# Attention and MLP on one Trainium2 core: batch 0's order, w_in's first half in blocks, two loads moved

## The chip, the core and the metric

The kernel runs on one core of one Trainium2 chip. A core has five engines that each run their own list of instructions in order: TensorE (PE in the profile; its weight loads are listed as PEld), VectorE (DVE), ScalarE (ACT), GpSimd (POOL) and SyncE (SP). They meet only where one waits for another's semaphore. Loads and stores are DMAs, issued by POOL, SP or ACT and carried out by the core's 16 DMA engines. The metric is the device time of one execution in microseconds (us); lower is better.

## The reference

Eight batches of eight heads, 512 local and 32 global tokens, head size 64. A local query sees the local keys within 32 positions and all 32 global keys; a global query sees all keys. The result of each head goes through a gated two-layer MLP of width 512, 2048, 512.

```
s_g = scale * q_g @ [k_g, k_l].T          ; out_g = softmax(s_g) @ [v_g, v_l]
s_l = [scale * q_l @ k_g.T, where(|i-j| <= 32, scale * q_l @ k_l.T, -1e9)]
out_l = softmax(s_l) @ [v_g, v_l]
x = concat([out_g, out_l], axis=2) -> (8 * 544, 512)
h = x @ w_in ; out = (h * sigmoid(1.702 * h)) @ w_out
```

## The kernel before

The types are bf16 with sums in f32 banks. Attention works on a *quad*: four heads of one batch side by side, so a batch has two quads; `a` is the first and `c` the second. A quad's work is a list of steps, each a method:

- `Tk`, `Tq` (L302, L309): VectorE turns the k and q loads into the layout that TensorE needs; `ext` puts the global queries beside them. q and k are loaded by `load(b, us, names)` (L74), where `us` names the quads of batch b.
- `B(rnd)` (L328): matmuls that write the band's bias into the banks of the scores; `S(rnd)` (L338): the score matmuls on top, in two rounds; `X(rnd)` (L375): ScalarE's exponentials into `E[rnd]`; `gg`, `K`, `XK`, `eg`: the same for the global tokens.
- `ekU(unit)`, `U(unit)` (L418, L429): three units of matmuls of the exponentials with ones (unit 0, the row sums) and with the two halves of v; `R` (L460) turns the row sums into reciprocals on VectorE; `XL(h)` (L470) multiplies units 1 and 2 by them and writes `xL`, the MLP's input. `Gm` and `G` do it for the global queries.
- `h_mm(i, fc, hp, kcs)` (L584): the MLP's first layer, one of 16 column blocks `fc` of w_in, in four parts `kc` of the contraction; parts 0 and 1 need quad a's xL, parts 2 and 3 quad c's. `h_step` adds the gate on ScalarE and VectorE (`th`, then `gT`); `o_mm` is the second layer.
- `zero(n, ...)` (L644): matmuls of zeros that add nothing to a bank; fillers.

Batches 1 to 7 use `Wide`, a variant of the quad with masks in place of the bias matmuls (`M`).

The order of the program (L651 on) is written out by hand, and each engine runs its share in this order. Batch 0 has nothing to overlap with but its own two quads. From L727 on, the h matmuls of batch 0 run, and later batches put their attention between the o matmuls of the batch before.

The loads of the early part are issued by POOL: L143 to L146 and L225 to L226 first, then `load_rest` (L248), called at L663, in this order: v of batch 0, constants, w_in in four blocks, w_out's quarters 1 and 0, the masks (on POOL itself), batch 1's first quad, its global tokens, its second quad, its global v, w_out's quarters 2 and 3, batch 2's first quad, batch 1's v, more global tokens. A w_in block of the before is one half of the columns (1,024) of one half of the rows; the rows of h part 0 and 1 are the first, those of 2 and 3 the second. Batch 2's second quad, v and later batches are loaded from L777 on.

`step` (L150), `ident`, `band` and `bias` (L195 to L197) are constants that a POOL select and three VectorE instructions make; the first bias matmuls need them.

Of the kernel before, what the change touches and what calls it, by code (L numbers as in the profile page):

```python
# [12 lines left out]
F32 = mybir.dt.float32  # L13
# [7 lines left out]
def kernel(  # L21
# [12 lines left out]
    nc = tc.nc  # L34
# [10 lines left out]
    NQ = B * 2  # L45
# [11 lines left out]
    consts = ctx.enter_context(tc.tile_pool(name="consts", bufs=1))  # L57
# [16 lines left out]
    def load(b, us=(0, 1), names="qk"):  # L74
        if b not in loaded:
            loaded[b] = (ld.tile([128, 2, 16 * D], BF16, name="rk"),
                         ld.tile([128, 2, 16 * D], BF16, name="rq"))
        s = slice(us[0], us[-1] + 1)
        for name in names:
            dst, src = ((loaded[b][0], kf), (loaded[b][1], qf))[name == "q"]  # L80
            nc.gpsimd.dma_start(out=dst[:, s], in_=src[b][:, s])
# [8 lines left out]
    def load_v(b):  # L90
        if b == 2:
            nc.gpsimd.memset(v_view(b, 5)[:, :, :, :, D:], 1.0)
        vt = v_view(b, 5).rearrange("p u j c d -> p (u j) c d")
        vs, vg = (x[b].rearrange("h s d -> s h d") for x in (v_l, v_g))
        for c in range(5):
            n = 128 if c == 2 else 96
            nc.gpsimd.dma_start(out=vt[0:n, :, c, :D], in_=vs[FIRST[c] : FIRST[c] + n])  # L97
            if c != 2 and b > 1:
                nc.gpsimd.dma_start(out=vt[96:128, :, c, :D], in_=vg)  # L99

    def load_vg(b):
        nc.gpsimd.dma_start(out=v_view(b, 5).rearrange("p u j c d -> p (u j) c d")[96:128, :, 0, :D],
                            in_=v_g[b].rearrange("h s d -> s h d"))

    def spread_vg(b):
        vt = v_view(b, 5).rearrange("p u j c d -> p (u j) c d")
        nc.vector.tensor_copy(vt[96:128, :, 1, :D], vt[96:128, :, 0, :D])
        nc.vector.tensor_copy(vt[96:128, :, 3:5, :D],
                              vt[96:128, :, 0:1, :D].to_broadcast([32, 8, 2, D]))
# [6 lines left out]
    def load_turned(eng, out_, in_):  # L116
        eng.dma_start(out=out_[32:128], in_=in_[0:96])
        eng.dma_start(out=out_[0:32], in_=in_[96:128])

    def load_g(lo, hi, names="kq"):  # L120
        for name, dst, src in (("k", rkg, kgf), ("q", rqg, qgf)):
            if name in names:
                nc.gpsimd.dma_start(out=dst[:, lo:hi, :], in_=src[:, lo:hi, :])
# [10 lines left out]
    def cast_g32(name, t):  # L134
        nc.vector.tensor_copy(t[:, 0:2, :D], g32[name])
# [5 lines left out]
    halves = (slice(0, 8 * D), slice(8 * D, 16 * D))  # L141
    load_g32("q", qgf)
    for f, eng in zip(halves, (nc.scalar, nc.sync)):  # L143
# [5 lines left out]
    nc.vector.memset(warm, 0.0)  # L149
    step = consts.tile([128, 289], BF16)  # L150
    nc.vector.memset(step, 1.0)
    nc.gpsimd.affine_select(
        out=step, in_=step, pattern=[[1, 289]], compare_op=ALU.is_ge,
        fill=0.0, base=-97, channel_multiplier=-1,
# [6 lines left out]
    def set_consts():  # L161
        nc.gpsimd.memset(ones32, 1.0)
        nc.gpsimd.memset(bd, 0.0)
        for j in range(4):
            r = (j + 1) % 4
            nc.gpsimd.memset(bd[32 * r : 32 * r + 32, j, :], 1.0)
        nc.gpsimd.memset(rvg[:, :, D:], 1.0)
        for i in range(2):
            nc.gpsimd.memset(v_view(i, 4 + i)[:, :, :, :, D:], 1.0)

    w_in_sb = wts.tile([128, 2, NKC, d_ff // 2], BF16)
    w_out_sb = wts.tile([128, FC, d_model], BF16)
    w_in_r = moe_w_in.rearrange("(u p h) f -> u p h f", u=2, h=2)
# [7 lines left out]
    for i in range(4):  # L181
        qt = consts.tile([128, 24, 32], F32, name="q%d" % i)
        nc.vector.memset(qt[:, 0:4, :], 0.0)
        nc.vector.memset(qt[:, 20:24, :], 0.0)
        qtiles.append(qt)

    WIN = ((0, 10), (6, 12), (14, 12), (22, 10))
    mask = consts.tile([128, 2, MW], BF16)
# [26 lines left out]
    def make_mask(part):  # L215
        rnd, at, t0, t1, nr, base, rows = part
        src = band[:, base : base + 16 * nr].rearrange("p (r t) -> p t r", t=16)
        nc.gpsimd.tensor_copy(mask_at(rnd, at, t1 - t0, nr)[0:rows], src[0:rows, t0:t1])

    def mask_rest():  # L220
        nc.gpsimd.memset(mask, 1.0)
        nc.gpsimd.memset(mask_at(0, 248, 16, 12)[96:128, :, 0:4], 0.0)
        nc.gpsimd.memset(mask_at(1, 236, 16, 12)[96:128, :, 8:12], 0.0)

    load(0, (1,), "kq")  # L225
    load_turned(nc.gpsimd, rvg[:, 0:2, :D], vgf[:, 0:2])  # L226

    qgT = consts.tile([128, NQ, 40], F32)
    nc.vector.memset(qgT[:, :, 32:], 0.0)
    kgT = consts.tile([128, NQ, 32], F32)  # L230
    def transpose_g(lo, hi, names="qk"):
        for name, dst, s in (("q", qgT, rqg), ("k", kgT, rkg)):
            if name not in names:
                continue
            nc.vector.transpose(dst[:, lo:hi, :32], s[:, lo:hi].bitcast(F32))

    def load_v2(b):
        vp = v_l[b].rearrange("(u h) (c p) d -> u p h c d", u=2, p=128)
        for u in range(2):
            for p in (slice(0, 64), slice(64, 128)):  # L240
                nc.gpsimd.dma_start(out=v_view(b, 4)[p, u, :, :, :D], in_=vp[u, p])

    def load_w_out(g4):
        nc.gpsimd.dma_start(
            out=w_out_sb[:, 4 * g4 : 4 * g4 + 4, :].rearrange("p (g e) m -> p g (e m)", e=2),
            in_=w_out_r[:, 2 * g4 : 2 * g4 + 2, :])

    def load_rest():  # L248
        load_v2(0)
        set_consts()  # L250
        half = d_ff // 2
        for part in range(2):
            for u in range(2):
                nc.gpsimd.dma_start(out=w_in_sb[:, part, 2 * u : 2 * u + 2, :],
                                    in_=w_in_r[u][:, :, part * half : (part + 1) * half])
        load_w_out(1)
        load_w_out(0)
        mask_rest()
        for part in MASKS:
            make_mask(part)  # L260
        load(1, (0,))
        load_g(2, 4)
        load(1, (1,))
        load_vg(1)
        load_w_out(2)
        load_w_out(3)
        load(2, (0,))
        load_v(1)
        load_g(4, 8)

# [10 lines left out]
    def bank(pair, j):  # L281
        return pair[j // 2][:, j % 2, :]
# [296 lines left out]
    def width(i):  # L579
        return TB if i < B else B * Sg  # L580
# [3 lines left out]
    def h_mm(i, fc, hp, kcs):  # L584
        for kc in kcs:
            nc.tensor.matmul(hp[:, : width(i)], lhsT=w_in_c[:, fc // 8, kc, fc % 8 // 2, :, fc % 2],  # L586
                             rhs=(xL[i] if i < B else xG)[:, kc, :],
                             start=(kc == 0), stop=(kc == NKC - 1))
# [53 lines left out]
    a, c = Quad(0), Quad(1)  # L642

    def zero(n, ps, m=128, w=512):  # L644
        for _ in range(n):
            nc.tensor.matmul(ps[:m, :w], lhsT=warm[:, :m], rhs=warm[:, :w], start=False, stop=False, skip_group_check=True)

    def cast_k(f):
        nc.scalar.activation(rk[:, 0, f], k32[:, f], AF.Copy)

    cast_k(halves[0])  # L651
    cast_g32("q", rqg)
    transpose_g(0, 2, "q")
    a.ext((0, 1), True)
    cast_k(halves[1])
    a.Tk(0, 8)
    a.Tq(0, 8)
    a.Tk(8, 16)
# [4 lines left out]
    load_rest()  # L663
    a.B(0)
    a.B(1, split=True)
    zero(34, a.bk[1][3], 32, 32)
    a.S(0, added=True, part=0)
    a.S(0, added=True, part=1)
    a.X(0)
    a.S(1, split=True, added=True)  # L670
    zero(3, a.bk[1][3])
    a.X(1)
    c.Tk()
    c.ext()
# [5 lines left out]
    c.gg()  # L680
    c.X(0)
    a.eg()
    a.ekU(0)
    a.U(0)
    a.R()
    c.K()
    c.XK()
    a.ekU(1)
    a.U(1)
    a.XL(0)  # L690
    c.B(1, js=(0, 1))
    c.B(1, js=(2, 3))
    c.S(1, added=True)
    c.X(1)
    a.ekU(2)
    a.U(2)
    a.XL(1)
    a.Gm()
    gTs[0] = moe.tile([128, FC, TB], BF16, name="gT")
    pt = pts[0] = spair()  # L700
    c.ekU(0)
# [3 lines left out]
    c.U(1)  # L705
    c.ekU(2)
    c.U(2)
    c.eg()
    for fc in range(4):
        h_mm(0, fc, bank(pt, fc), (0, 1))  # L710
    c.XL(0)
    c.XL(1)
    for kc in (2, 3):
        for fc in range(4):
            h_mm(0, fc, bank(pt, fc), (kc,))
# [21 lines left out]
    nq = {b: (Wide(2 * b), Wide(2 * b + 1)) for b in (1, 2)}  # L737
    a, c = nq[1]
# [11 lines left out]
    a.S(1)  # L750
    a.X(1)
    spread_vg(1)
    nq[2][0].Tq()
    a.M(1)
    nq[2][0].Tk()
    osteps(0, (1, 2), (2, 2))
# [17 lines left out]
    a.G()  # L774
    transpose_g(4, 6)
    nq[2][0].ext(nc.gpsimd)
    load(2, (1,))  # L777
    load_v(2)
    load(3)
    osteps(0, (3, 2), (3, 3))  # L780
    a, c = nq[2]
# [4 lines left out]
    for fc in range(FC):  # L786
        if fc < 2:
            h_act(1, fc, hps[fc])
        else:
            h_step(1, fc)  # L790
        if fc == 1:
            nq[1][1].G()
        if fc == 10:
            a.S(0)
            a.X(0)
            a.M(0, nc.gpsimd)
            load_v(3)
            load(4)
            load_g(8, NQ)
# [101 lines left out]
```

## Time and profile before

| what | us |
|---|---|
| three runs, median (lowest to highest) | 299.2 (299.19 to 299.46) |
| the profiled execution, its own time | 299.52 |
| its span in the profile | 297.7 |
| TensorE busy | 291.9 |
| VectorE busy | 219.1 |
| ScalarE busy | 165.0 |
| GpSimd busy | 79.7 |

The span runs from the first to the last instruction that the profile shows; the profiled execution took 1.8 us more than it. An idle engine costs time only where the chain that ends last waits for it. "Idle before" gives how long the engine stood still before an instruction, and the arrow what ended this. The start of a load's row is its issue; "to landing" counts from there to the time that all its data are in place.

### The profile page before, as it was taken

To read this page: it belongs to the slowest core of one execution; us is meant where nothing else is said; L and a number is where in the kernel's file an instruction comes from. 1 tells how busy PE (TensorE), PEld (TensorE's weight loads), DVE (VectorE), ACT (ScalarE), POOL (GpSimd) and SP (SyncE) were. 2 spreads that over 40 slices of the span, in tenths; PEclk is the share of its full clock that TensorE was granted. 3 is DMA by queue.
4 is the path that set the end of the run, shared out by engine and by line. 5 is a ranking of instruction groups with operands and counts; after the bars stand their busy time and mean duration, and the time that the engine had idled before them with its cause. 6 is when DMAs were issued, how large, how long until landed. Compare 5 with 4: busy or idle time off the path is not lost.

```text
span 297.7 us, 8197 instructions
## 1 busy us (share of the span) xinstructions
PE 291.9 (98%) x3444; PEld 149.5 (50%) x3444; DVE 219.1 (74%) x440; ACT 165.0 (55%) x251; POOL 79.7 (27%) x130
## 2 busy tenths in 40 slices
PE   8999999999999999999999999999999999999995
PEld 5544446445454455445454455445554455446654
DVE  6669988869867887788878887778877866683320
ACT  3827375585557745567456655666446651663421
POOL 8962730589563002700072003500000000000000
PEclk9999999999999999999999999999999999999999
DMA  7999997699999213981299014901120022101122
GB/s 157 168 206 211 204 186 105 120 142 153 167 197 184 47 37 66 140 134 29 47 99 192 12 41 84 112 0 39 36 70 4 2 46 65 35 2 35 35 64 79
DMA packets 58228, 27.93 MB, mean 94 GB/s; under 512 B 47312, under 2 KB 47824, under 8 KB 58192
## 3 DMA queue, kind: packets, MB, share of 16 engines
q0 software_dynamic: 50784, 17.83, 53.2%
q1 hardware_dynamic: 7264, 9.31, 12.2%
q8 instruction: 27, 0.44, 0.6%
q10 hardware_dynamic: 144, 0.26, 0.3%
q14 instruction: 9, 0.07, 0.1%
HBM read 36.31 MB, written 8.91 MB: 152 GB/s over the span
## 4 chain that ended last, share of the span: by engine, by line
PE 96%; ACT 1%; DVE 1%; issue 0%
PE op L611 39%; PE hp L586 38%; PE s L531 6%; PE ov L557 5%; PE op L623 1%; PE w L178 1%; PE s L335 1%; PE og L568 1%; PE ov L438 1%; PE s L586 1%; ACT e L380 1%; ACT e L385 1%; DVE xL L471 0%; PE ov L426 0%; PE s L352 0%; PE s L557 0%
## 5 line engine op out<-in xcount | busy, mean ns | idle before, releaser
L611 PE MATMUL op<-w_out_sb,gT 128*128 128x512 bf16 x528 | 121.7, 379 | 0.0
L594 DVE SCALAR_TENSOR_TENSOR gT<-th,hp 128x512 bf16<-128x512 f32 (+1 forms) x140 | 91.2, 657 | 40.6 <-ACT th L593 39.7
L586 PE MATMUL hp<-xL,w_in_sb 128*128 128x512 bf16 x496 | 108.7, 379 | 0.0
L593 ACT ACTIVATE th<-hp 128x512 f32<-128x512 f32 (+1 forms) x140 | 79.8, 573 | 42.8 <-PE hp L586 40.9
L586 PEld LDWEIGHTS <-w_in_sb 128*128 128x128 bf16 x576 | 56.0, 98 | 64.9 <-DMA w_in_sb<-in_moe_w_in_dram 0.8
L611 PEld LDWEIGHTS <-gT 128*128 128x128 bf16 x528 | 49.3, 98 | 54.9
L542 ACT ACTIVATE e<-s 128x1016 bf16<-128x1016 f32 (+1 forms) x56 | 53.3, 1004 | 7.4 <-PE s L531 7.1
L626 ACT ACTIVATE ob<-op 128x512 f32<-128x512 f32 x32 | 18.9, 599 | 62.9 <-PE op L611 62.9
L97 POOL DMA_DIRECT2D v<-in_v_l_dram x35 | 28.4, 815 | 83.5 <-PE og L568 81.9
L547 DVE TENSOR_TENSOR e<-e,mask 128x1712 bf16<-128x1712 bf16 (+1 forms) x27 | 28.3, 1049 | 3.3 <-ACT e L542 3.3
L462 DVE STREAM_TRANSPOSE sT<-ov 128x512 f32<-128x512 f32 x15 | 10.7, 716 | 14.7 <-PE ov L557 12.6
L471 DVE TENSOR_TENSOR xL<-ov,rs 128x512 bf16<-128x512 f32 x30 | 19.4, 686 | 1.9 <-PE ov L438 0.5
L531 PE MATMUL s<-q,kT 32*128 32x160 bf16 (+3 forms) x672 | 19.2, 243 | 0.0
L531 PEld LDWEIGHTS <-kT 32*128 32x128 bf16 x672 | 13.1, 94 | 12.0 <-issue 6.5
L505 DVE STREAM_TRANSPOSE kT<-rk 128x512 f32<-128x512 f32 x14 | 14.5, 1033 | 0.0
L99 POOL DMA_DIRECT2D v<-in_v_g_dram x24 | 14.3, 595 | 0.0
L310 DVE STREAM_TRANSPOSE q<-rq 128x512 f32<-128x512 f32 (+1 forms) x17 | 11.5, 675 | 0.9 <-DMA rq<-in_q_l_dram 0.9
L466 DVE STREAM_TRANSPOSE rs<-rT 128x512 f32<-128x512 f32 x16 | 11.4, 711 | 0.6
L557 PE MATMUL ov<-e,v 128*32 128x128 bf16 (+3 forms) x624 | 11.7, 223 | 0.0
L557 PEld LDWEIGHTS <-v 128*32 128x32 bf16 x672 | 10.5, 97 | 0.0
L586 PE MATMUL hp<-xG,w_in_sb 128*128 128x256 bf16 x64 | 9.6, 273 | 0.0
L557 PE MATMUL ov<-e,ones 128*32 128x128 bf16 (+3 forms) x312 | 7.1, 225 | 0.0
(102 smaller groups left out, 156.3 us busy)
## 6 DMA issues: line engine op xcount, KB each, us to landing
out_dram<-ob SPq DMA_DIRECT2D x128, 64.0 KB, 1.7
v<-in_v_l_dram POOLq DMA_DIRECT2D x28, 96.0 KB, 4.4
rq<-in_q_l_dram POOLq DMA_DIRECT2D x5, 512.0 KB, 7.2
rk<-in_k_l_dram POOLq DMA_DIRECT2D x5, 512.0 KB, 9.3
w_in_sb<-in_moe_w_in_dram POOLq DMA_DIRECT2D x4, 512.0 KB, 10.5
w_out_sb<-in_moe_w_out_dram POOLq DMA_DIRECT2D x4, 512.0 KB, 12.0
v<-in_v_l_dram POOLq DMA_DIRECT2D x11, 128.0 KB, 4.7
rk<-in_k_l_dram POOLq DMA_DIRECT2D x5, 256.0 KB, 9.9
```

The costliest lines, as they stand in the source:

```text
L97: nc.gpsimd.dma_start(out=vt[0:n, :, c, :D], in_=vs[FIRST[c] : FIRST[c] + n])
L471: nc.vector.tensor_mul(self.x[:, 2 * self.u + h, :], self.st[1 + h], self.st["rs"])
L505: nc.vector.transpose(flat[:, 0:Sl].rearrange("p (r t) -> p t r", t=16), loaded[self.b][0][:, self.u].bitcast(F32))
L531: nc.tensor.matmul(bank(self.ps, j)[:, at : at + n], lhsT=self.k[p, KEYS[c] : KEYS[c] + 128, e], rhs=self.q[p, lo:hi, r0 : r0 + nr, e], st ...
L542: nc.scalar.activation(self.E[rnd][:, 2 * i : 2 * i + 2, :n], self.ps[i][:, :, :n], AF.Exp, scale=scale)
L547: eng.tensor_mul(e, e, mask[:, rnd : rnd + 1, :n].to_broadcast([128, 4, n]))
L557: nc.tensor.matmul(ov[32 * j : 32 * j + 32, :].rearrange("p (t r) -> p t r", t=16)[:, t0:t1, r0 : r0 + nr], lhsT=lv, rhs=self.E[rnd][:, j, ...
L586: nc.tensor.matmul(hp[:, : width(i)], lhsT=w_in_c[:, fc // 8, kc, fc % 8 // 2, :, fc % 2], rhs=(xL[i] if i < B else xG)[:, kc, :], start=( ...
L593: nc.scalar.activation(th[:, :n], hp[:, :n], AF.Tanh, scale=0.851)
L594: nc.vector.scalar_tensor_tensor(gTs[i][:, fc, :n], in0=th[:, :n], scalar=1.0, in1=hp[:, :n], op0=ALU.add, op1=ALU.mult)
L611: nc.tensor.matmul(op, lhsT=gTs[i][:, fc, tci * 128 : tci * 128 + 128], rhs=w_out_sb[:, fc, :], start=(first and fc == 4 * f4), stop=(fc = ...
L626: nc.scalar.activation(ob, op, AF.Copy, scale=0.5)
```

## The change

Eight edits, in the order of the program:

1. c's k is loaded before the select that makes `step`, its q where both were.
2. `qgT`'s memset stands before the constants.
3. w_in's first column half is loaded in two blocks of 512 columns for each half of the rows, so there are six loads in place of four.
4. `load_w_out(2)` stands ahead of batch 1's second quad.
5. q of batch 2's first quad is loaded (on POOL) and turned (on VectorE) later: behind `ext` of that quad, and behind fc 6 of batch 1's h steps.
6. The second half of k is cast before ext; the 34 small fillers are split into 6, 14 and 14 at three places.
7. `c.K` goes ahead of a's unit 0; the first half of `c.B(1)` ahead of `a.ekU(1)`; `a.U(1)` and `a.XL(0)` behind `c.X(1)`.
8. `a.Gm` goes behind the first h matmuls, `c.eg` behind `c.XL`.

```
     step = consts.tile([128, 289], BF16)
     nc.vector.memset(step, 1.0)
+    load(0, (1,), "k")
     nc.gpsimd.affine_select(
...
+    qgT = consts.tile([128, NQ, 40], F32)
+    nc.vector.memset(qgT[:, :, 32:], 0.0)
+
     WIN = ((0, 10), (6, 12), (14, 12), (22, 10))
...
-    load(0, (1,), "kq")
+    load(0, (1,), "q")
     load_turned(nc.gpsimd, rvg[:, 0:2, :D], vgf[:, 0:2])
-    qgT = consts.tile([128, NQ, 40], F32)
-    nc.vector.memset(qgT[:, :, 32:], 0.0)
...
-        for part in range(2):
+        for part, lo, hi in ((0, 0, half // 2), (0, half // 2, half), (1, 0, half)):
             for u in range(2):
-                nc.gpsimd.dma_start(out=w_in_sb[:, part, 2 * u : 2 * u + 2, :],
-                                    in_=w_in_r[u][:, :, part * half : (part + 1) * half])
+                nc.gpsimd.dma_start(out=w_in_sb[:, part, 2 * u : 2 * u + 2, lo:hi],
+                                    in_=w_in_r[u][:, :, part * half + lo : part * half + hi])
...
         load_g(2, 4)
+        load_w_out(2)
         load(1, (1,))
         load_vg(1)
-        load_w_out(2)
         load_w_out(3)
-        load(2, (0,))
+        load(2, (0,), "k")
...
     cast_k(halves[0])
+    cast_k(halves[1])
     cast_g32("q", rqg)
     transpose_g(0, 2, "q")
     a.ext((0, 1), True)
-    cast_k(halves[1])
...
-    zero(34, a.bk[1][3], 32, 32)
+    zero(6, a.bk[1][3], 32, 32)
     a.S(0, added=True, part=0)
+    zero(14, a.bk[1][3], 32, 32)
     a.S(0, added=True, part=1)
     a.X(0)
     a.S(1, split=True, added=True)
     zero(3, a.bk[1][3])
+    zero(14, a.bk[1][3], 32, 32)
     a.X(1)
...
     a.eg()
+    c.K()
     a.ekU(0)
     a.U(0)
     a.R()
-    c.K()
     c.XK()
+    c.B(1, js=(0, 1))
     a.ekU(1)
-    a.U(1)
-    a.XL(0)
-    c.B(1, js=(0, 1))
     c.B(1, js=(2, 3))
     c.S(1, added=True)
     c.X(1)
+    a.U(1)
+    a.XL(0)
     a.ekU(2)
     a.U(2)
     a.XL(1)
-    a.Gm()
...
     c.U(2)
-    c.eg()
     for fc in range(4):
         h_mm(0, fc, bank(pt, fc), (0, 1))
+    a.Gm()
     c.XL(0)
     c.XL(1)
+    c.eg()
...
     spread_vg(1)
-    nq[2][0].Tq()
     a.M(1)
...
     nq[2][0].ext(nc.gpsimd)
+    load(2, (0,), "q")
     load(2, (1,))
...
             nq[1][1].G()
+        if fc == 6:
+            a.Tq()
         if fc == 10:
```

More of the change, by code (lines that the diff above doesn't have):

```diff
@@ L151 @@
     nc.vector.memset(step, 1.0)
+    load(0, (1,), "k")
     nc.gpsimd.affine_select(
@@ L185 @@
         qtiles.append(qt)
+    qgT = consts.tile([128, NQ, 40], F32)
+    nc.vector.memset(qgT[:, :, 32:], 0.0)
     WIN = ((0, 10), (6, 12), (14, 12), (22, 10))
@@ L223, in mask_rest @@
         nc.gpsimd.memset(mask_at(1, 236, 16, 12)[96:128, :, 8:12], 0.0)
-    load(0, (1,), "kq")
+    load(0, (1,), "q")
     load_turned(nc.gpsimd, rvg[:, 0:2, :D], vgf[:, 0:2])
-    qgT = consts.tile([128, NQ, 40], F32)
-    nc.vector.memset(qgT[:, :, 32:], 0.0)
     kgT = consts.tile([128, NQ, 32], F32)
@@ L251, in load_rest @@
         half = d_ff // 2
-        for part in range(2):
+        for part, lo, hi in ((0, 0, half // 2), (0, half // 2, half), (1, 0, half)):
             for u in range(2):
-                nc.gpsimd.dma_start(out=w_in_sb[:, part, 2 * u : 2 * u + 2, :],
-                                    in_=w_in_r[u][:, :, part * half : (part + 1) * half])
+                nc.gpsimd.dma_start(out=w_in_sb[:, part, 2 * u : 2 * u + 2, lo:hi],
+                                    in_=w_in_r[u][:, :, part * half + lo : part * half + hi])
         load_w_out(1)
@@ L262, in load_rest @@
         load_g(2, 4)
+        load_w_out(2)
         load(1, (1,))
         load_vg(1)
-        load_w_out(2)
         load_w_out(3)
-        load(2, (0,))
+        load(2, (0,), "k")
         load_v(1)
@@ L651 @@
     cast_k(halves[0])
+    cast_k(halves[1])
     cast_g32("q", rqg)
@@ L654 @@
     a.ext((0, 1), True)
-    cast_k(halves[1])
     a.Tk(0, 8)
@@ L665 @@
     a.B(1, split=True)
-    zero(34, a.bk[1][3], 32, 32)
+    zero(6, a.bk[1][3], 32, 32)
     a.S(0, added=True, part=0)
+    zero(14, a.bk[1][3], 32, 32)
     a.S(0, added=True, part=1)
@@ L671 @@
     zero(3, a.bk[1][3])
+    zero(14, a.bk[1][3], 32, 32)
     a.X(1)
@@ L682 @@
     a.eg()
+    c.K()
     a.ekU(0)
@@ L685 @@
     a.R()
-    c.K()
     c.XK()
+    c.B(1, js=(0, 1))
     a.ekU(1)
-    a.U(1)
-    a.XL(0)
-    c.B(1, js=(0, 1))
     c.B(1, js=(2, 3))
@@ L694 @@
     c.X(1)
+    a.U(1)
+    a.XL(0)
     a.ekU(2)
@@ L697 @@
     a.XL(1)
-    a.Gm()
     gTs[0] = moe.tile([128, FC, TB], BF16, name="gT")
@@ L707 @@
     c.U(2)
-    c.eg()
     for fc in range(4):
         h_mm(0, fc, bank(pt, fc), (0, 1))
+    a.Gm()
     c.XL(0)
     c.XL(1)
+    c.eg()
     for kc in (2, 3):
@@ L752 @@
     spread_vg(1)
-    nq[2][0].Tq()
     a.M(1)
@@ L776 @@
     nq[2][0].ext(nc.gpsimd)
+    load(2, (0,), "q")
     load(2, (1,))
@@ L792 @@
             nq[1][1].G()
+        if fc == 6:
+            a.Tq()
         if fc == 10:
```

## The prediction

> **What bounds the kernel now.** I read the page's busy times and slices first, then the chain of waits in order of time, then the timeline of the first 30 us, then the landings of the loads tile by tile.
>
> ```profile
> PE 291.9 (98%) x3444; PEld 149.5 (50%) x3444; DVE 219.1 (74%) x440; ACT 165.0 (55%) x251; POOL 79.7 (27%) x130
> PE   8999999999999999999999999999999999999995
> DMA  7999997699999213981299014901120022101122
> ```
>
> TensorE is busy 98% of the span, so from some early point on the kernel is a fixed pile of matmuls. Time can be won only ahead of that point, by starting the pile sooner, or lost behind it, by opening a hole. The chain tells where the point is (start, length, what):
>
> ```profile
> 7.94 1.64 ACT e L385 x2
> 9.58 1.71 ACT e L380 x4
> 11.29 0.50 ACT ek L416
> 11.79 0.04 issue
> 11.83 0.40 PE ov L426 x4
> ...
> 13.63 0.71 PE s L335 x8
> 14.34 0.59 PE s L352 x16
> ...
> 17.05 0.73 DVE sT L462
> ...
> 18.10 0.71 DVE rs L466
> 18.81 0.12 DVE eg L397
> 18.93 1.29 DVE xL L471 x2
> 20.21 0.02 issue
> 20.23 1.90 PE s L586 x8
> 22.13 0.27 PE og L456 x17
> 22.40 10.63 PE hp L586 x48
> ```
>
> Until 20.23 the chain changes engines: exponentials of a's scores, a's units, c's second scores, c's row sums on VectorE, xL. From 20.23 it is TensorE alone, but for one hole of 0.54 us at 50.8 to 51.4 that the trace lays to "issue". So the sum is: how much sooner do the matmuls of 20.23 start, and does a load or VectorE open a hole behind them? Two things hold that start at once:
>
> ```profile
> 18.73 0.18 DVE L397 TENSOR_TENSOR eg<-bd,e 128x128 bf16<-128x128 bf16 x1
> 18.91 1.29 DVE L471 TENSOR_TENSOR xL<-ov,rs 128x512 bf16<-128x512 f32 x2
> 20.22 1.41 PEld L586 LDWEIGHTS <-w_in_sb 128*128 128x128 bf16 x8 [0.82 <-DMA w_in_sb<-in_moe_w_in_dram]
> 20.23 1.90 PE L586 MATMUL s<-xL,w_in_sb 128*128 128x512 bf16 x8 [0.33 <-DVE xL L471]
> ```
>
> xL ends at 20.20, and w_in's second load lands at 20.18. Winning on one alone would win nothing.
>
> **The start (k of c sooner, q memset, cast order).** POOL's k load of c takes 0.57 and now stands before the select that makes `step` (0.46), so ident, band and bias come some 0.55 later: bias ends near 4.47, not 3.93. Bias matmuls then start at 4.50, not 4.23. Their 16 take 2.10 here, the first ten at a slow rate (0.13 to 0.16 apart), the last six fast (0.07 to 0.09); the fast rate begins near 5.7. If it does so again, fewer are slow and they end at about 6.3 as before. The memset moved off VectorE's path gives back 0.17 of the 0.55; the q path waits for its load anyway (Tq at 5.64 and 6.91, both released by DMA). The second cast of k now precedes ext on ACT: its data land at 4.85, it ends near 5.48, ext near 5.9, and part 0 needs them at 6.6. Nothing. c's q is issued no sooner (same work before it on POOL), so c.Tq stays at 10.0.
>
> **Fillers.** 34 small ones took 1.01, 0.025 apart, and a.S(0) queued behind them from 7.21. Part 0 needs only kT, ended at 6.57; with 6 fillers it runs at 6.60, 14 more end near 7.25, part 1 waits for Tq (7.36) and starts at 7.39 instead of 7.47. So ACT's exponentials start 0.07 sooner, and ACT is busy without a break to 13.42: **-0.07** carried to c.X(0)'s end, 13.35. The 14 behind zero(3) fill TensorE's wait for a.X(0) (0.43 between the second and third bias matmul at 9.2 to 9.6).
>
> **Units reordered.** From c.gg (11.36) to c.X(1) (14.98) are 3.62 us. New order, spacings from the timeline: gg 0.10, K 0.44 (now in the hole before 11.83), ekU(0) 0.32, U(0) 0.42, two bias blocks 0.35, ekU(1) 0.32, the other two 0.35, c.S(1) to its end 0.70: 3.00. One wait: the second bias pair needs c.X(0)'s bank at 13.35 and stands there at 13.31, with the release 0.07. So c.X(1) starts at 14.43: **-0.55**. What left the path, a.U(1) (0.42), now runs beside c.X(1) (1.66 on ACT) with ekU(2), U(2) and c's ekU(0), ekU(1), some 1.7 together: just hidden. c.U(0), R, U(1), U(2) follow as now, 0.55 sooner; the first h matmuls start at 17.45, not 18.00.
>
> **eg behind xL; a.Gm behind the first h matmuls.** eg (0.18) leaves VectorE's path: xL ends at 20.20 - 0.55 - 0.18 = 19.47. TensorE: 8 x 0.216 from 17.45 is 19.18, a.Gm adds 0.37 (as c.Gm does at 21.75 to 22.34), 19.55. The later holds: **19.55 instead of 20.23, -0.68**, if w_in is there. a.Gm came out of the window before 15.8, where c.X(1) hides its place.
>
> **w_in in blocks.** POOL keeps eight loads in flight: its 20th issue waits at 20.46 for the 12th landing, the 21st and 22nd for the 13th and 14th. Loads land in order, 2.45 apart per full block:
>
> ```profile
> L254 POOL DMA_DIRECT2D w_in_sb<-in_moe_w_in_dram x4: 696/710/715, 9.7 to 11.8; - x4
> DMA to landing us min/median/max: 7.8/10.5/13.1
> ```
>
> that is 17.50, 20.18, 22.41, 24.90 for the four. With halves first, the two that the first four fc need land near 16.6 and 18.0, ahead of 17.45 and 19.55. But a row of 512 columns is a packet of 1,024 bytes, and a packet took 98 ns where 2,048 bytes took 173 (the packet records): 196 for 173, 13% more on two blocks, 0.33 each, so every later landing moves by **+0.66**. Bounds: 0 (bytes alone) and 5.2 (the two q loads of the head, 128 such packets each, landed 1.27 apart; four half blocks of 256 would take 10.2, not 4.9 - but those two shared the engines with two other queues). I take 0.66. The Trainium skill (DMA: Bandwidth & Descriptors, Specifications) puts full rate at 512 bytes and up, by which this would be 0 and the time 0.04 less; the packet rows speak against it. The last half block: 24.90 + 0.66 = 25.56, released 0.04 later; fc 8's third matmul stood at 26.24 and would stand at 25.56: **+0.04**. This was 1.3 us of slack and is now none. The two extra issues (1.4 on POOL) and the eight-in-flight rule push the masks to about 19.7; first use 40.
>
> **w_out's third quarter sooner.** It lands at 38.09 now and would at 36.0; its use moves from 38.9 to 38.2, so it stays hidden. Batch 1's second k goes from 35.34 to about 38.45. Then c.Tk, Tq, ext end at 40.8, needed by c.S(0) at 41.7; a.M(0) slips to 40.8, and the Tq taken out behind it (0.70) brings M(1) back to 43.7, needed at 45.8. Nothing. Batch 1's last v lands at 46.90 + 0.66 - 1.25 (q of batch 2, now behind) = 46.3, needed at 47.14 - 0.64 = 46.5. Without q's move it would be late.
>
> **q of batch 2 later.** Issued behind ext on POOL, near 55.2; the load in this place took 4.5 us to land, so 59.7. a.Tq (0.70) stands in VectorE behind fc 6, at 60.2. VectorE idles 0.17 of each 0.86 there and four hp banks give TensorE 1.8 us of cover: nothing.
>
> **Sum:** -0.68 + 0.04 = -0.64; the profiled 299.52 becomes 298.88, and against the median of 299.2 (0.32 less, as now) 298.56.
>
> **Rivals.** (1) *The w_in blocks bind.* For: no slack at 25.56. Against: q0's packets run back to back, so only their own length counts. Each us over 0.66 is lost in full; with 0.3 to 0.7 more the gain is 0 to 0.35, 298.85 to 299.2. (2) *The slow rate of TensorE lasts longer*, since the bias matmuls leave a hole of 0.27 at 4.23. Seven matmuls of 128x512 took 3.17 (627 ns each) where the same shape takes 383 at 8.5. The slow rate lasted from 1.26 to 5.7, 4.4 us; if that begins anew at 4.5, it lasts to 8.9, bias, part 0, fillers and part 1 take twice their time, S(0) ends 1.0 later, and the chain with it: 299.56. The Trainium skill (TensorE: Matmul & The Clock Gate, Part 1: The HAM clock gate) has a free-running window of some 3.4 us that opens the clock once it was busy; by it a hole of 0.27 is small, and no run here shows where its bound lies. (3) *Slower: q of batch 2 is late.* If it lands after 61.5, gT of fc 7 comes too late for TensorE's fc 11 and a.S(0) at 62.3 waits too. The q load of 75.3 took 7.2, which gives 62.4, 0.9 of stall and 299.4; the page's median for such a load, 9.1, gives 64.3, 2.8 of stall and **301.3**. Against: the queue has run empty there (DMA share 0.39 of 4 us in 52 to 56). (4) *The hole at 51 goes too.* Nothing that TensorE waits for is named there; if it hangs on what the loads do just then, it may close: 0.54 more, 298.0, or open elsewhere.
>
> **Numbers.** Forecast 0.53, its own range 298.2 to 298.9. (1) 0.15, (2) 0.05, (3) and other new holes 0.12, (4) closing 0.15. A measurement of this kernel can tell about 0.2% (0.6 us) from no change; the forecast lies just past it, so some 0.68 of its chance counts as faster: 0.36 + 0.15 = 0.51. Same: 0.17 + 0.15 + 0.05 = 0.37, less 0.02 for blocks that cost more than the slack: 0.35. Slower 0.14. The range reaches to (4) and to a mild (3): 297.8 to 299.8.
>
> **What would show it.** a.X(0) at 7.85; c.X(1) at 14.4 (not 15); xL's end near 19.5; no wait on w_in before it; hp from 21.7; a wait of PEld on w_in near 25.6 of 0.1 or less; a.Tq of batch 2 near 60.2 with no DMA wait. Wrong if c.X(1) starts after 14.8, if PEld waits for w_in over 0.4 us, or if the chain shows a DVE or DMA entry after 22.

## The result: a little slower

| | forecast | measured |
|---|---|---|
| median, us | 298.56 (297.8 to 299.8) | 299.72 (299.40 to 302.39, 20 runs) |
| the kernel before, beside it | | 299.20 (298.60 to 300.07, 20 runs) |
| ratio | 0.998 | 1.0024, 95% interval 1.0014 to 1.0035 |

The changed kernel is about 0.7 us slower by the ratio. The profiled execution doesn't show it: its span is 297.7 as before, but that execution of the kernel before took 299.52, 0.32 over its median. The page of the profile after, busy times and slices of TensorE:

```profile
PE 291.4 (98%) x3444; PEld 148.9 (50%) x3444; DVE 219.2 (74%) x440; ACT 165.1 (55%) x251; POOL 81.1 (27%) x132
PE   6999999999999999999999999999999999999995
```

The pile is as dense as before, and only the first slice got emptier (6 for 8 tenths). So the answer lies ahead of the pile again. The chain of waits of the profile after, up to 23 us (start, length, what):

```profile
1.33 5.15 DMA rq<-in_q_l_dram
...
7.92 0.45 PE s L648 x14
8.37 0.41 PE s L354 x14
8.78 1.64 ACT e L387 x2
...
18.54 1.83 PE s L588 x8
20.38 0.28 PE og L458 x18
20.65 1.84 PE s L588 x8
22.49 0.28 PE og L458 x20
```

Two things are new on it. The 14 fillers (L648) stand in the chain itself, between the two parts of the scores, and a.Gm (L458 at 20.38) stands between the two halves of the first h matmuls. There is no VectorE entry behind 7.5 any more, and still nothing was won. The marks, from the records of each instruction (kc2 is the first h matmul of part 2, hp the first matmul of the next fc):

| us | forecast | before | before, a second profile | after | after, a second profile |
|---|---|---|---|---|---|
| first, second half of q landed | 5.6, 6.9 | 5.62, 6.89 | 5.87, 6.91 | 6.48, 7.39 | 5.94, 7.05 |
| a.X(0) starts | 7.85 | 7.92 | 7.89 | 8.76 | 8.48 |
| c.X(1), behind a.X(0) | 6.58 | 7.06 | 7.05 | 6.64 | 6.65 |
| kc2, behind a.X(0) | 11.70 | 12.31 | 11.81 | 11.83 | 11.83 |
| hp, behind a.X(0) | 13.9 | 14.42 | 13.91 | 13.94 | 14.11 |

Above the line of a.X(0) the head lost 0.6 to 0.8. Below it the order won 0.4 at c.X(1), and at kc2 all of that is gone, if the second profile of the kernel before is the measure; against the first, 0.48 is left. c.X(1) in the timelines of before and after:

```profile
14.98 1.66 ACT L385 ACTIVATE e<-s 128x856 bf16<-128x856 f32 x2 [1.07 <-PE s L352]
```

```profile
15.40 1.66 ACT L387 ACTIVATE e<-s 128x856 bf16<-128x856 f32 x2 [0.66 <-PE s L354]
```

Behind hp the two kernels are alike: from hp to the start of the last matmul it is 271.41 and 271.43 after, 271.80 and 271.55 before. The first profile of before has its hole of 0.54 at 51; the second hasn't.

### The profile page after: what moved, and what is told of

It is laid out like the page before. It is cut to its first block, busy times and chain, and to the rows that moved or that the text cites. A ratio compares the mean times of both kernels' runs of the same rounds, so it can differ in the third digit from the quotient of the medians.

```text
span 297.7 us, 8199 instructions
## 1 busy us (share of the span) xinstructions
PE 291.4 (98%) x3444; PEld 148.9 (50%) x3444; DVE 219.2 (74%) x440; ACT 165.1 (55%) x251; POOL 81.1 (27%) x132
## 4 chain that ended last, share of the span: by engine, by line
PE 94%; ACT 2%; DMA 2%; DVE 0%; issue 0%; POOLq 0%
PE op L613 39%; PE hp L588 38%; PE s L533 6%; PE ov L559 5%; DMA rq<-in_q_l_dram 2%; PE s L588 1%; PE op L625 1%; ACT e L387 1%; PE ov L440 1%; PE og L570 1%; ACT e L382 1%; PE s L354 0%; PE s L559 0%; PE ov L428 0%; PE og L458 0%
## 5 line engine op out<-in xcount | busy, mean ns | idle before, releaser
L81 POOL DMA_DIRECT2D rk<-in_k_l_dram x10 | 6.4, 636 | 3.0 <-DMA w_out_sb<-in_moe_w_out_dram 1.9
```

## The experiments

Four theories. The **early k**: c's k load, ahead of the select, makes the first loads of q land later. The **fillers**: the 14 between the parts of the scores hold up the second part. The **units**: the new order gives its gain back. The **blocks**: the loads of w_in hold up the first h matmuls. The rival to all is that a profile or a median happened to fall so. Ratios are to the kernel before, run on the same chip in the same call.

### Both kernels looked at once more

`after_again` and `before_again` are the two kernels with nothing edited.

> The changed kernel once more, for a second profile. Theory K: the first q half lands near 6.5 again. Rival R: it lands somewhere else between 5.5 and 6.5.

> The kernel before once more, for a second profile. Theory K: the first q half lands near 5.6 again. Rival R: it lands somewhere between 5.5 and 6.5. Apart from the theories: if the hole of 0.54 us at 51 us is there again, it belongs to this program; if not, it is chance.

One run each: 299.41 and 298.74. Their marks stand in the table. The first half of q landed at 5.94 and 5.87, so theory K missed both, and the landing scatters as the rival had it. The timeline of the kernel before in its second profile (start, length, engine, line, operation; in brackets the idle time before and what ended it):

```profile
18.19 3.40 PE L586 MATMUL s<-xL,w_in_sb 128*128 128x512 bf16 x15 [0.16 <-issue]
...
18.87 1.29 DVE L471 TENSOR_TENSOR xL<-ov,rs 128x512 bf16<-128x512 f32 x2
19.64 1.46 PEld L586 LDWEIGHTS <-w_in_sb 128*128 128x128 bf16 x8 [0.27 <-DMA w_in_sb<-in_moe_w_in_dram]
...
21.52 0.32 PE L456 MATMUL og<-v,e 128*32 128x66 bf16 x16
```

The h matmuls run without a break (one of 16 records is missing, the first, whose weights load at 17.96). Part 2 starts at 19.70, while xL isn't complete until 20.16: it needs only the first of the two products of xL, which ends at 19.56. In the profile that the forecast was made from, the only thing that held part 2 was w_in's landing at 20.18, a wait of 0.5, and here w_in lands at 19.59 and holds nothing. Which of the two is usual, these profiles don't say. The four other profiles with w_in in whole blocks (e2, e4, e5 and e10 below) all have the wait: it costs TensorE 0.23 to 0.46 there, 0.49 in the first profile of before.

### The early k

`e1_k_back` is the kernel after with c's k load back (its edit stands below), `e2_k_early_alone` the kernel before with it early:

```
-    load(0, (1,), "k")
     nc.gpsimd.affine_select(
...
-    load(0, (1,), "q")
+    load(0, (1,), "kq")
```

> The changed kernel with c's k load put back behind the select; all else as changed. Theory K (the early k load slows the loads already under way, so that batch 0's first q half lands 0.86 late and everything behind it starts late): the first q half lands near 5.6 us, Tq starts at 5.6 to 5.8, a.X(0) at 7.9, hp starts at 21.7 to 21.9, time 298.4 to 298.9, ratio 0.997 to 0.999. Rival R (that late landing is chance of one profile, and the loss lies in the order of the units, the fillers or the w_in blocks): time as the changed kernel, 299.5 to 299.9. Rival C (the bias matmuls start later and the slow rate of TensorE lasts longer in some runs): no run with a granted clock under 0.995 here, but the median as the changed kernel's.

> The kernel before, with c's k load ahead of the select and nothing else changed. Theory K: the first q half lands at 6.3 to 6.6, Tq is released then, hp starts at 23.0 to 23.3, time 299.8 to 300.1, ratio 1.002 to 1.003. Rival R: q lands at 5.6, time 299.1 to 299.3. Rival C: q lands at 5.6, the median is unmoved, but some runs have a granted clock under 0.995 and are 1 to 3 us longer.

e1: 299.41, ratio 1.0009 (0.9996 to 1.0023). e2: 299.47, 1.0008 (0.9999 to 1.0017). Both point to the early k, neither is clear of no change, and both times lie between what the theory and what its rival gave. The halves of q landed at 6.17 and 7.10 in e1's profile and at 7.38 and 8.20 in e2's. `e10_k_early_spaced` put a pause on POOL ahead of the early load, in e2:

```
+    pause = consts.tile([128, 440], BF16)
+    nc.gpsimd.memset(pause, 0.0)
     load(0, (1,), "k")
```

> The kernel before with c's k ahead of the select, as in e2_k_early_alone, but with a memset on POOL ahead of k that takes about as long as the select did, so that k is issued near 3.0 as before and the select ends 0.4 later still. Theory K (what slows the first q halves is that k follows them too closely): first q half lands at 5.3 to 6.2, time 299.0 to 299.4. Rival (the late select and bias matmuls cost the time): 299.5 or more, with q in time. Rival (the landing scatters by itself): first q half anywhere between 5.3 and 7.4.

299.48, 1.0007 (0.9998 to 1.0015). q landed at 5.79 and 6.57, not late, but all that POOL issues behind came some 0.45 later too (the bias matmuls start at 4.93, w_in's second load lands at 20.39), so it tells nothing apart.

### The fillers

`e4_fillers_alone` is the kernel before with the fillers split as the change has it, `e3_k_and_fillers_back` is e1 with them as before (the edit below):

```
-    zero(6, a.bk[1][3], 32, 32)
+    zero(34, a.bk[1][3], 32, 32)
     a.S(0, added=True, part=0)
-    zero(14, a.bk[1][3], 32, 32)
     a.S(0, added=True, part=1)
...
-    zero(14, a.bk[1][3], 32, 32)
```

> The changed kernel with c's k back behind the select and the fillers as before (34 ahead of a.S(0), none between its parts, none behind the three large ones); loads, units, xL and cast order stay changed. Theory F (the 14 fillers between the parts of a.S(0) hold part 1 up, because kT ends near 7.1 in most executions and not at 6.6, and the moved fillers leave TensorE idle ahead, so that in some executions the clock falls back for 3.4 us): a.X(0) starts 0.5 behind the end of the second q turn (not 0.9), time 298.7 to 299.1, no run with a granted clock under 0.996. Rival O (the order of the units and the loads lose the time): time 299.3 to 299.6 as with k alone put back, a.X(0) no sooner.

> The kernel before with the fillers split into 6, 14 and 14, nothing else changed. Theory F: a.X(0) starts 0.9 behind the end of the second q turn instead of 0.5, time 299.5 to 299.8 (ratio 1.001 to 1.002), and one run in ten or so has a granted clock near 0.994 and is 1.5 to 2.7 longer. Rival O: no change, 299.1 to 299.4.

e3: 299.59, 1.0015 (1.0005 to 1.0025); e4: 299.25, 1.0007 (0.9999 to 1.0016). e3 is a miss: with both edits of the head undone it is still slower than before, and no better than e1. e4's time is in its rival's range. What the fillers do shows in the traces all the same. The timeline of before, then of the profile after:

```profile
6.26 1.01 PE L646 MATMUL s<-warm 128*32 128x32 bf16 x34
6.91 0.45 DVE L310 STREAM_TRANSPOSE q<-rq 128x256 f32<-128x256 f32 x1 [0.34 <-DMA rq<-in_q_l_dram]
...
7.21 1.18 PE L352 MATMUL s<-q,kT 32*128 32x120 bf16 x48
...
7.92 1.66 ACT L385 ACTIVATE e<-s 128x856 bf16<-128x856 f32 x2 [2.19 <-PE s L352]
```

```profile
5.84 0.32 PE L648 MATMUL s<-warm 128*32 128x32 bf16 x6
6.50 0.45 DVE L312 STREAM_TRANSPOSE q<-rq 128x256 f32<-128x256 f32 x1 [1.11 <-DMA rq<-in_q_l_dram]
6.87 0.57 DVE L308 STREAM_TRANSPOSE kT<-rk 128x256 f32<-128x256 f32 x1
7.41 0.45 DVE L312 STREAM_TRANSPOSE q<-rq 128x256 f32<-128x256 f32 x1
...
7.50 0.42 PE L354 MATMUL s<-q,kT 32*128 32x120 bf16 x16 [1.34 <-DVE kT L308]
...
7.85 0.52 PE L648 MATMUL s<-warm 128*32 128x32 bf16 x14
...
8.30 0.92 PE L354 MATMUL s<-q,kT 32*128 32x80 bf16 x32
...
8.76 0.88 ACT L387 ACTIVATE e<-s 128x856 bf16<-128x856 f32 x1 [3.12 <-PE s L354]
```

The second turn of q ends at 7.86, and the second score part could run then. In front of it stand 14 fillers until 8.30: a.X(0) comes 0.90 behind the turn. TensorE meanwhile had stood idle for 1.34, since part 0 waits for kT, which VectorE turns behind the first half of q. Before, the fillers were all done ahead of both parts, and this distance is 0.56 and 0.51 in the two profiles of the kernel before. Over all profiles with the split it is 0.89 to 1.07 (five), without it 0.51 to 0.69 (eleven of thirteen; 0.85 in e3 and 1.67 in g4, where TensorE's granted clock became full only at 6.5 and 6.8 and the 34 fillers ran late). The other 14, behind `zero(3)`, cost little: c.X(0) starts 3.70 to 3.72 behind a.X(0) in the five, 3.67 or 3.68 in eleven without (3.98 and 4.34 in e6 and e9, where c's q landed late).

### The units

`e5_units_alone` is the kernel before with edits 7 and 8:

```
+    c.K()
     a.ekU(0)
     a.U(0)
     a.R()
-    c.K()
     c.XK()
+    c.B(1, js=(0, 1))
     a.ekU(1)
-    a.U(1)
-    a.XL(0)
-    c.B(1, js=(0, 1))
     c.B(1, js=(2, 3))
     c.S(1, added=True)
     c.X(1)
+    a.U(1)
+    a.XL(0)
...
-    a.Gm()
...
-    c.eg()
     for fc in range(4):
         h_mm(0, fc, bank(pt, fc), (0, 1))
+    a.Gm()
     c.XL(0)
     c.XL(1)
+    c.eg()
```

> The kernel before with the units of batch 0 reordered (c.K, c.B(1), a.U(1), a.Gm, c.eg), nothing else. Theory G (a.Gm now stands on TensorE's path and gives back the 0.4 that c.X(1) gains; eg costs xL nothing where it stood): c.X(1) starts 0.4 sooner behind a.X(0) (6.64 instead of 7.06), the first h matmul 0.4 to 0.6 sooner, but the hp matmuls only 0 to 0.1 sooner where w_in's second load does not bind: time 299.0 to 299.3. As forecast before the change: 0.5 sooner, if w_in does not bind: 298.7. Rival O: slower, 299.4 or more.

299.25, 1.0003 (0.9994 to 1.0011): nothing. c.X(1) starts 6.64 behind a.X(0), as in the kernel after, so the order does win its 0.42 there. The timeline of e5 shows where it stops:

```profile
20.46 1.90 PE L586 MATMUL s<-xL,w_in_sb 128*128 128x512 bf16 x8 [0.39 <-DMA w_in_sb<-in_moe_w_in_dram]
```

### The blocks of w_in

`e6_loads_alone` is the kernel before with edits 3 to 5; `e7_loads_own_tiles` is e6 with a tile of its own for each column block:

```
-    w_in_sb = wts.tile([128, 2, NKC, d_ff // 2], BF16)
+    w_lo = wts.tile([128, NKC, d_ff // 4], BF16)
+    w_hi = wts.tile([128, NKC, d_ff // 4], BF16)
+    w_in_sb = wts.tile([128, NKC, d_ff // 2], BF16)
...
-                nc.gpsimd.dma_start(out=w_in_sb[:, part, 2 * u : 2 * u + 2, lo:hi],
-                                    in_=w_in_r[u][:, :, part * half + lo : part * half + hi])
+                nc.gpsimd.dma_start(out=w[:, 2 * u : 2 * u + 2, :], in_=w_in_r[u][:, :, lo:hi])
```

> The kernel before with the load edits alone (w_in's first half in blocks, w_out's third quarter sooner, q of batch 2 later). Theory F with G: nothing is late, and the wait for w_in's second load ahead of the third h matmul (0 to 0.3 by the two profiles of before) is gone: 298.9 to 299.2. Rival O or rival 1 of the prediction (the blocks bind): a wait on w_in near 25.6 or on v near 46.5, 299.4 to 299.8.

> The load edits alone, as in the run e6_loads_alone, but with w_in's two column blocks in tiles of their own, so that no h matmul of the first four fc waits for the second blocks. Theory W (in one tile the reads of kc 1 and kc 3 overlap the span that the second blocks' writes cover, so the kernel waits for all four block loads and the edit loses what it was to win): no wait of PEld on w_in between 17 and 23, hp 13.9 behind a.X(0) (14.4 in e6_loads_alone), time 0.2 to 0.4 under e6_loads_alone: 298.7 to 299.0. Rival (the second blocks are not what is waited for, their place in the queue is): a wait of PEld on w_in stays near 20 to 21.5, time 299.1 to 299.3.

e6: 299.16, 0.9998 (0.9985 to 1.0010). e7: 299.37, 1.0001 (0.9991 to 1.0011). In time they are alike, and e7 misses the time that its theory gave, though its hp comes 13.92 behind a.X(0) as forecast (14.41 in e6). e6's timeline has a wait that its forecast ruled out:

```profile
20.30 0.53 PEld L586 LDWEIGHTS <-w_in_sb 128*128 128x128 bf16 x3 [0.18 <-issue]
...
21.58 0.55 PEld L586 LDWEIGHTS <-w_in_sb 128*128 128x128 bf16 x4 [0.75 <-DMA w_in_sb<-in_moe_w_in_dram]
```

The blocks that the first four fc read had landed by then; at 21.54 it is the *other* column block of the same rows that lands. The semaphores that e6's weight loads wait for say the same: those of part 0 wait for the 11th load of the queue and those of part 2 for the 12th, which are theirs, but those of part 1 for the 13th and those of part 3 for the 14th, the blocks beside them. That is what follows if, in one tile, a block's write counts as the whole stretch from its first to its last column over both of the parts kc that it fills: the low block of the second part lies inside the stretch of the high one. e7 bears it out. In the kernel after the 14th landing is at 20.77 and part 3 starts late enough; in its second profile it cost 0.16 (21.19 to 21.35). With tiles of their own this wait is gone from e7, e8, e9 and g2 to g4. The load edits win no time even so: e7 has no wait ahead of hp and is as fast as the kernel before. `e9_changed_own_tiles` is e3 with these tiles:

> The changed kernel with c's k and the fillers put back, as in e3_k_and_fillers_back, and w_in's column blocks in tiles of their own. Theory W and G together: hp 13.94 behind a.X(0) as in e3 (there the second blocks landed in time), time 0 to 0.2 under it: 299.2 to 299.6, so not under before. Rival (the waits for the second blocks cost most of it): 298.8 or less.

299.20, 1.0002 (0.9991 to 1.0013). The time is under the kernel after, not under before. The mark was missed: hp came 14.53 behind a.X(0) and c.X(1) 7.23, since c's q landed only at 11.18 (9.97 in the profile of before) and c's first scores waited 0.75 for its turn. So this profile doesn't tell theory from rival.

### a.Gm in a hole: the version that beats both

If the units give their gain back through a.Gm, which now stands on TensorE's path with 0.3 (20.30 to 20.59 in the profile after), it must go where TensorE waits anyway. `e8_own_tiles_gm_sooner` is e7 with the new order of the units, fillers and k as before, and a.Gm with the first part of a.G ahead of the second half of c's bias, which waits for c.X(0)'s bank:

```
     c.B(1, js=(0, 1))
     a.ekU(1)
+    a.Gm()
+    a.G(1)
     c.B(1, js=(2, 3))
...
-    a.G()
+    a.G(2)
     c.Gm()
```

> The run e7_loads_own_tiles and the changed order of batch 0's units, but with a.Gm ahead of the second pair of c.B(1), where TensorE waits for c.X(0)'s bank, and with the part of a.G that frees its bank ahead of a.XL(0). Fillers and c's k as before the change. Theory G (a.Gm behind the first h matmuls gave back the gain): hp starts 13.5 to 13.7 behind a.X(0), time 298.4 to 298.8, ratio 0.997 to 0.999. Rival (VectorE's or ScalarE's chain to xL bounds, not TensorE): hp 13.9 behind a.X(0), time as e7_loads_own_tiles.

298.82, 0.9988 (0.9977 to 0.9999): faster than both. Run again beside the next three as `g4_best_again`:

> e8 once more, the base of g2 and g3 on the same chip: 298.7 to 299.0, a ratio of 0.998 to 0.9995 to the kernel before. If its gain was chance: 1.000.

298.92, 0.9988 (0.9979 to 0.9996). The timeline of g4:

```profile
13.79 0.32 PE L457 MATMUL og<-v,e 128*32 128x66 bf16 x16
...
14.07 0.48 PE L336 MATMUL s<-bias,ident 128*128 128x192 bf16 x4
...
15.18 1.66 ACT L386 ACTIVATE e<-s 128x856 bf16<-128x856 f32 x2 [0.80 <-PE s L353]
...
18.25 3.63 PE L596 MATMUL s<-xL,w_lo 128*128 128x512 bf16 x16
...
22.08 0.61 PE L596 MATMUL hp<-xL,w_hi 128*128 128x512 bf16 x2
```

a.Gm at 13.79 costs c.X(1) 0.15 (6.79 behind a.X(0) at 8.39, for 6.64), and the 16 h matmuls run in one piece. hp comes 13.70 behind a.X(0) in all four profiles that have this order (e8, g2, g3, g4), against 13.94 in the four profiles of the changed order that have no wait for w_in in front (after, e1, e3, g1) and 13.91 and 13.92 in the old order without that wait (before's second profile, e7).

### k and fillers, once more, on two bases

`g1_fillers_back` is the kernel after with e3's edit of the fillers alone; `g2_best_k_early` is e8 with the early k; `g3_best_fillers_split` is e8 with e4's edit.

> The kernel after with the fillers as before (all 34 ahead of batch 0's first score part), nothing else undone; c's k stays early. If the split fillers cost the time, by standing 0.44 us in front of the second score part: 299.3 to 299.5, a ratio of 1.0003 to 1.0010 to the kernel before, with a.X(0) 0.5 us behind the end of the second turn of q. If the early load of k costs it: no change from the kernel after, near 299.7 (1.0015 to 1.0025). If it is neither alone but the clock of TensorE falling back in some executions of the changed kernel: a median near 299.3 with single runs above 301.

> e8 with c's k load ahead of the select, as the change has it, and nothing else. If the early k makes the first halves of q land later (6.6 us on average over three profiles with it, 5.9 over ten without): 0.0010 to 0.0025 above the ratio of e8 in this call. If its queue place is worth nothing: equal to e8 within 0.0008.

> e8 with the fillers split 6, 14 and 14 around the first two score parts, as the change has it, and nothing else. If the split costs: a.X(0) 0.9 us behind the end of the second turn of q rather than 0.5, and 0.0005 to 0.0015 above the ratio of e8 in this call. If it costs nothing: equal to e8 within 0.0005.

g1: 299.66, 1.0011 (1.0001 to 1.0021). By its median it is where the early k alone would put it, by its ratio between the two; no run is above 300.38. g2: 299.27, 1.0000 (0.9990 to 1.0009), 0.0012 above g4. g3: 299.17, 0.9994 (0.9984 to 1.0004), 0.0006 above g4. Both differences are what the costs would give, but with intervals of some 0.0009 either way neither stands clear by itself. g1's timeline is the clearest picture of the early k:

```profile
5.85 1.01 PE L648 MATMUL s<-warm 128*32 128x32 bf16 x34
7.52 0.45 DVE L312 STREAM_TRANSPOSE q<-rq 128x256 f32<-128x256 f32 x1 [1.88 <-DMA rq<-in_q_l_dram]
...
7.89 0.57 DVE L308 STREAM_TRANSPOSE kT<-rk 128x256 f32<-128x256 f32 x1
8.47 0.45 DVE L312 STREAM_TRANSPOSE q<-rq 128x256 f32<-128x256 f32 x1
8.51 1.36 PE L354 MATMUL s<-q,kT 32*128 32x120 bf16 x45 [1.65 <-DVE kT L308]
...
9.43 0.88 ACT L387 ACTIVATE e<-s 128x856 bf16<-128x856 f32 x1 [3.77 <-PE s L354]
```

All of the head hangs on q's landing, and here its first half is 1.9 later than in the profile of before. Over the profiles, the second half of q landed at 7.05 to 8.45 with the early k (five, mean 7.71), and at 6.25 to 7.39 without (twelve, mean 6.96; e10, with its pause, is left out). c's k itself came no sooner for being issued 0.46 sooner: it landed at 9.02 on average over the five, at 8.52 over the twelve.

### All ratios together

Six edits, switched on or off in 14 measurements (all but e10, with g4 as a second one of e8). If their costs simply add, least squares over the 14 ratios, each weighted by its interval, gives these estimates (twice the standard error behind them; the worst, e3, is off by 0.0008):

| edit | us |
|---|---|
| early k | +0.25 ± 0.17 |
| fillers split | +0.18 ± 0.17 |
| units and a.Gm as in the change | +0.13 ± 0.20 |
| load edits 3 to 5, w_in in one tile | +0.09 ± 0.23 |
| w_in in three tiles | -0.10 ± 0.29 |
| a.Gm sooner | -0.45 ± 0.29 |

The first four add up to 0.65 us, and 0.0024 of 299.2 is 0.72. Only the early k, the split fillers and a.Gm's new place stand clear of zero. One rival was never switched alone: the memset of `qgT` (edit 2) and the order of k's casts stand in after, e1, e3, e9 and g1 and in no other kernel. With a seventh term for these two the first two rows stay as they are, the seventh is +0.09 ± 0.40, and a.Gm sooner becomes -0.38 ± 0.40, no longer clear of zero. So its gain is shown by the traces (13.70 for 13.94 at hp) and by e8 and g4 against the kernel before, and its size is open.

## Why the prediction was wrong

**The step that failed.** The text had the matmuls of part 2 start 0.68 sooner, at 19.55 for 20.23; they started at 20.59 and 20.31. Two terms of the sum failed. The head was put at "nothing" for the early k and -0.07 for the fillers. But a.X(0) came at 8.76 and 8.48 for 7.85, and the ratios give these two +0.25 and +0.18, together 0.43 of the 0.72. And the -0.68 of the units was counted from a start that w_in had held back by 0.5; with a.Gm on TensorE's path nothing is left of it against a start that waits for nothing. The ratios give the units +0.13 ± 0.20 and the load edits +0.09 ± 0.23, so where the rest of the 0.72 comes from stays open.

**What bounds the kernel: half right.** Time was lost ahead of the pile, as the text said it must be. But "two things hold that start at once" was wrong. xL held nothing: part 2 needs the first of its two products, which ended at 19.60 in that profile. Only w_in held it, by 0.5. So most of the -0.68 was measured from a wait for a load, and such a wait scatters: it is gone in the second profile of before and 0.23 to 0.46 in e2, e4, e5 and e10. How much of it a usual execution has stays open: five of the six profiles with whole blocks have it, but e7, which is rid of it, is no faster (1.0001).

**The units: -0.55 was -0.42,** right in kind. The path got shorter as worked out, the second bias pair with its wait included. (The text's own terms, 13.35 with 0.07, 0.35 and 0.70, add up to 14.47 and not 14.43, which is nearer to what came.)

**eg: -0.18 was 0.** Where eg stood, xL started 18.91 with the row sums' last turn (18.10, 0.71) ending at 18.81; after, the turn ends at 19.29 and xL starts at 19.40. Its 0.18 overlapped what xL needs anyway, and xL wasn't on the path.

**a.Gm: why the order won nothing.** The text added its 0.37 to a TensorE that ran until 19.18, and let the later of two ends hold; against a start of 20.23 that looked free. Against the gapless 11.81 behind a.X(0) it takes back the whole gain: 11.83. Measured, the gain at the first h matmul is 0.37 (9.71 behind a.X(0); before, second profile: 10.08 by its weight load), and a.Gm adds 0.37 between the h matmuls, just as the text had it. So its size was right; wrong was the start that it was set against. With a.Gm in a hole (e8) hp comes 0.24 sooner (13.70 for 13.94), and the ratios find -0.45 ± 0.29.

**The fillers: -0.07 was +0.18 by the ratios** and 0.4 in the traces. Part 1 isn't held by q alone but by the 14 fillers. The text put part 0 and the 14 between the end of kT (6.57) and the end of q's second turn (7.36), 0.79 later. They take 0.80 in the profile after (7.50 to 8.30). In 11 of the 17 other profiles there is only 0.25 to 0.54 between the two ends (0.42 in the profile after), so the 14 stand in front of part 1.

**The early k: "Nothing" was +0.25.** Its place on POOL was costed: 0.57, and the 0.27 at bias, measured 4.54 for 4.23. No run has that delay without the early k, so it isn't shown by itself whether it cost nothing, as the text said. The loads of q that were in flight beside it were not. That they land later with it is what the profiles show (7.71 for 6.96 on average); what in the queues does it wasn't settled.

**The blocks: right for the wrong reason.** The first two low blocks landed at 15.93 and 17.19, sooner than the 16.6 and 18.0 forecast, and the last half block at 25.86 for 25.56. (Over twelve profiles with the blocks the last load of w_in landed at 25.97 on average, over six without at 25.14: 0.83 later for the text's 0.66. The packets' length doesn't explain it: in the profile after three half blocks landed 1.26 and 1.24 apart, half of a whole block's 2.47 in the profile of before, and the fourth 2.34 behind the third. What held the fourth wasn't settled.) "The two that the first four fc need" was false in one tile. Rival 1, the blocks that bind, came true in small. It cost TensorE 0.42 in e6 (its weight loads waited 0.75), 0.16 in the second profile of after, and 0.48 at the last block of w_in in g3:

```profile
26.68 1.41 PEld L596 LDWEIGHTS <-w_in_sb 128*128 128x128 bf16 x8 [0.81 <-DMA w_in_sb<-in_moe_w_in_dram]
```

**Right: w_out, batch 1, q of batch 2.** a.Tq of batch 2 starts at 60.73 with no wait for its load (59.77; forecast 59.7 and 60.2), c.Tk of batch 1 waits 1.25 for its k and nobody for it, and v of batch 1 lands at 46.16 (46.3). Rival 3 didn't come. **The hole at 51** is gone after, as rival 4 had it, but it is gone in the second profile of before too, so nothing was won by it. The slow matmuls of rival 2 did not last in the profile after, where the granted clock is full from 4.06. In the second they lasted to 7.07, but so they did in e4 and e6 (7.21, 7.31), which lack the hole that the rival hangs on.

## What to carry to other kernels

A gain is measured from what holds the path, and a wait for a load can be 0.5 in one execution and nothing in the next: profile the kernel before several times before building on a wait of half a microsecond. An instruction that is moved out of a hole must be costed on the engine it lands on once that engine has no holes left: a.Gm took back what the order had won, and the version with a.Gm in another hole is the one that was faster than both. And a filler belongs where the engine waits in every execution; between two parts of the critical work it turns into work as soon as a load comes a little later.

## What the runs showed of the hardware

- The first loads scatter. The second half of q landed between 6.25 and 8.45 over 17 profiles. a.X(0), and all behind it, moved with it where neither the split fillers nor a late clock (e3, g4) stood between.
- TensorE's granted clock became full between 4.03 and 7.31 over all 18 profiles. The Trainium skill (TensorE: Matmul & The Clock Gate, Part 1: The HAM clock gate) has a free-running window of some 3.4 us and a transition that varies by 0.5 us either way. The spread here is 3.3.
- Three of the 20 executions of the kernel after ran at a mean granted clock of 0.989 to 0.994 and took 301.44 to 302.39, one of 12 of e1 at 0.994 and 301.2; in no other kernel did it fall below 0.998. Both have the split fillers, but so have e4 and g3, and none of their 23 executions fell, so what does it isn't shown. They don't make the verdict: without the three the median is 299.70.
- Some copies on VectorE wait for POOL's DMA issues. Over all 18 profiles 54 copies of 128x192 start while POOL issues a DMA; 13 of them take 0.35 to 0.62 for the usual 0.26, and all 13 end 0.05 to 0.09 behind the issue. Of 198 that start outside an issue one takes longer. The timeline of e3:

```profile
34.12 1.55 POOL L97 DMA_DIRECT2D v<-in_v_l_dram  x2
...
35.29 0.48 DVE L508 COPY kT<-kT 128x192 f32<-128x192 f32 x1
...
36.50 0.88 POOL L97 DMA_DIRECT2D v<-in_v_l_dram  x1 [0.82 <-DMA w_out_sb<-in_moe_w_out_dram]
...
36.86 0.55 DVE L521 COPY kT<-kgT 128x128 f32<-128x128 f32 x1
...
37.47 0.32 PE L532 MATMUL s<-q,kT 32*128 32x160 bf16 x8 [0.20 <-DVE kT L521]
```

The copies of 0.48 and 0.55 end 0.09 and 0.03 behind POOL's issues; where the first starts as POOL's issue ends (35.74 and 35.76 in the profile after), it takes 0.26. In e3 it opened a hole of 0.20 on TensorE, in e6 of 0.34. The Trainium skill (SBUF — State Buffer, SBUF: two separate sides) has a pair of ports that VectorE and GpSimd share, locked for a whole instruction. The rows agree.
